# Three edits to the order of weight writes, output sums and x splits in the second MoE layer

## The chip, the cores and the metric
The kernel runs on 1 core of one Trainium2 chip. The metric is the device time of a run in microseconds (us). Before the change it is 1165.81 us, the median of 3 runs (1162.89 to 1167.37).

## The reference
Three stages follow each other, all in float32: a retention attention on 4 x 8 heads of 768 steps, a first MoE layer with w_in and w_out, and a second MoE layer with a gate. The change touches the second layer only (3072 tokens, 512 features, 1536 hidden):

```python
def _moe2_ref(x, w_gate, w_val, w_out):
    gate = 1.0 / (1.0 + np.exp(-(x @ w_gate)))
    val = x @ w_val
    return (gate * val @ w_out).astype(np.float32)
```

## The kernel before
**Precision.** TensorE (PE) multiplies a reduced form of float32. Each operand is therefore split into a high part `h` (a rounding copy on ACT) and a low part `l` (raw minus `h`, a subtraction on DVE or POOL), and each product is three matmuls: h times h, h times l, l times h.

**Seven products instead of eight.** A block of the gate or value product is cut into 2 x 2 quarters and computed with seven products of sums (a Strassen-Winograd scheme). The operands A11, A12, S1 to S4, A22 are weight quarters and their sums; B11, B21, B22, B12 and T1 to T4 are quarters of x and their differences. `product()` is one of the seven: six matmuls of 128 x 128 by 512 columns. One block is a *chain*: `begin(n)` runs A11 B11 into bank `pa` and lets ACT copy the bank to `m` (L707); `middle(n)` runs A12 B21 into `pb`, S2 T2 onto `pa` (ACT copies it to `u`, L725), S1 T1 into `pd`, S3 T3 onto `pa` (copied again, L737); `finish(n)` runs A22 T4 and S4 B22. PE works on `pa` again only when ACT has copied it.

**Groups.** The 3072 tokens are three groups of 1024. A group has twelve chains: three rounds r of two pairs p, each with a gate chain (m = 0) and a value chain (m = 1); over the rounds the six pairs q count the output weights. Group 0 (L1163) also makes the weights: `load_chain(n)` loads raw weights (L563, SP queue), `sums(n)` forms S1 to S4 on POOL (L569 to L573), `split_chain` splits them (ACT L608, DVE or POOL L609), and `keep_chain(n)` writes the four split tiles (`oh`, `ol`, early and late) to the scratch tensor `wcd` (L591), from where the groups 1 and 2 load them (L600). The tiles of a chain alternate between two sets, so a split for chain n+2 overwrites those of chain n. `load_out` loads w_out blocks (L775, two buffers `wor`), `split_out2` splits them (ACT L781, POOL L782).

**Outputs.** At the end of a round PE runs the output products; beside them `keep_out` writes split output weights, and generators on the list `todo`, made by `out_sums(q)`, load two raw w_out blocks of pair q (L808), form four quarter sums on POOL (L804), split them (ACT L822, DVE L823) and write them to `wtd` (L826). Groups 1 and 2 load them from there with `load_wt` (L834).

**x of the next group.** `prep_x(g)` is a generator that loads eight quarters of x, forms the differences T1 to T4 on POOL (L525) and splits all of them, `h` on ACT (L529), `l` on DVE, the one of T4 on POOL (L530). It is stepped at the last pair of a group, inside the last chain and between the output products. The split tiles of x exist once, so the splits wait for the old group's last products.

**What sets the order.** Each engine, and SP with its DMA queue, works its instructions off in program order, and waits at one hold everything behind it. The order is written out by hand, by the place of the calls and by stepping generators. In the lists of order below, the lines of the changed program are some 50 higher (L591 is L642, L563 is L614, L775 is L826, L608 is L659, L822 is L873, L707 is L758).

Of the kernel before, what the change touches and what calls it, by code (L numbers as in the profile page):

```python
# [8 lines left out]
F32 = mybir.dt.float32  # L9
F32R = mybir.dt.float32r  # L10
# [3 lines left out]
ALU = mybir.AluOpType  # L14

P = 128
# [9 lines left out]
def retention_moe_moe2(  # L26
# [12 lines left out]
    nc = tc.nc  # L39
# [420 lines left out]
    B11, B21, T2, T1, T3, T4, B22, B12 = range(8)  # L460
    chains = [(g, r, p, m) for g in range(NG) for r in range(NR) for p in range(PAIRS) for m in range(2)]
    NC0 = 2 * PAIRS * NR
    QS = PAIRS * NR
# [3 lines left out]
    p2 = {}  # L467
# [28 lines left out]
    def prep_x(g):  # L496

        hl = [
            [p2["x"].tile([P, 2, 512], F32R, name=f"{n}{j}", tag=f"{n}{j}") for n in ("xoh", "xol")] for j in range(7)
        ]  # L500
        xo[g] = hl
        raws = [{}, {}]

        def load(k, *js):
            for j in js:
                half, kk = {B11: (0, k), B12: (1, k), B22: (1, k + 2), B21: (0, k + 2)}[j]
                name = "xu" if g and k and j != B21 else "xt"
                raws[k][j] = p2[name].tile([P, 512], F32, name=name, tag=name)
                nc.sync.dma_start(out=raws[k][j], in_=x2d[2 * g + half][:, kk, :])

        load(0, B11, B12, B22, B21)
        if g:
            load(1, B11, B12, B22)
        yield
        for k in range(2):
            raw = raws[k]
            if k:
                if not g:
                    load(1, B11, B12, B22, B21)
                    yield  # L520
            for j in (T1, T2):
                raw[j] = p2["xt"].tile([P, 512], F32, name="xt", tag="xt")

            def diff(j, a, b):
                nc.gpsimd.tensor_tensor(out=raw[j], in0=raw[a], in1=raw[b], op=ALU.subtract)  # L525

            def split(j, engine):
                h, l = hl[j]
                nc.scalar.copy(h[:, k, :], raw[j])  # L529
                engine.tensor_tensor(out=l[:, k, :], in0=raw[j], in1=h[:, k, :], op=ALU.subtract)  # L530

            diff(T1, B12, B11)
            split(B11, nc.vector)
            if g and not k:
                load(1, B21)
            yield
            diff(T2, B22, T1)
            split(B21, nc.vector)
            yield
            raw[T3] = raw[B12]  # L540
            diff(T3, B12, B22)
            split(T2, nc.vector)
            yield
            raw[T4] = raw[B21]
            diff(T4, B21, T2)
            split(T1, nc.vector)
            yield
            split(T3, nc.vector)
            yield
            split(T4, nc.gpsimd)  # L550
            split(B22, nc.vector)
            yield

    wraw8, wo = {}, {}

# [31 lines left out]
    def keep_chain(n):  # L587

        for late in (False, True):
            for t, sl in parts[n, late]:  # L590
                nc.sync.dma_start(out=wcd[n][:, sl, :], in_=t.bitcast(F32))  # L591
# [118 lines left out]
    def middle(n):  # L710

        a, m1 = cb[n]
        b, d = bank2("pb"), bank2("pd")
        ahead = n + 1 < NC0
        if ahead and (n + 1) not in early:
            early[n + 1] = split_chain(n + 1, False)
        product(n, b, A12, B21, True, True)
        add(b, b, m1)
        while carried:
            next(carried.pop())  # L720
        c11 = consume(n, 0, b)
        next(c11)
        product(n, a, S2, T2, False, True)
        u2 = tmp("u2", 1)
        nc.scalar.copy(u2, a)  # L725
        if whole:
            whole.pop()
            split_out2()
        next(c11)
        if ahead:  # L730
            early.pop(n + 1)()
        pump()
        product(n, d, S1, T1, True, True)
        product(n, a, S3, T3, False, True)
        u3, c22 = tmp("u3", 1), tmp("c22", 1)
        pump()
        nc.scalar.copy(u3, a)  # L737
        next(c11)
        add(c22, d, u3)
        pump()  # L740
        cb[n] = [a, d, u2, c22]
# [200 lines left out]
    with tc.manual_schedule():  # L942
# [220 lines left out]
        for n, (g, r, p, m) in enumerate(chains[:NC0]):  # L1163
            last = 2 * p + m == 2 * PAIRS - 1
            more = n + 1 < NC0
            keep_chain(n)
            load_chain(n + 2)
            if more:
                load_out(n + 1)
            else:  # L1170
                load_split(n + 1)
            if not last and r == NR - 1 and p == PAIRS - 1:
                xs = prep_x(g + 1)
                next(xs)
            middle(n)
            if n + 2 < NC0 and not (last and r == NR - 1):
                sums(n + 2)
            if last:
                for _ in range(2):
                    next(xs, None)  # L1180
            if not last:
                begin(n + 1)
                rest = split_chain(n + 1, True)
                finish(n, False)
                rest()
                whole.append(n)
                continue
            rest = split_chain(n + 1, True) if more else lambda: None
            split_out2()
            ob = {}  # L1190
            for tt in range(2):
                ob[tt] = bank2("po")
                out_products(ob[tt], tt, range(2))
            finish(n, True)
            rest()
            if not more:
                load_split(n + 2)
            ob[2] = bank2("po")
            out_products(ob[2], 2, range(2))
            keep_out(r)  # L1200
            if r < NR - 1:
                todo.extend(out_sums(q) for q in ((0, 1), (2, 3, 4))[r])
            for tt in range(TOK):
                if tt >= 3:
                    ob[tt] = bank2("pd" if tt < 5 else "po")
                out_products(ob[tt], tt, range(0 if tt >= 3 else 2, FR))
                evict(g, r, tt, ob[tt])
                if tt < TOK - 1:
                    next(xs, None)
                    next(xs, None)  # L1210
                for _ in range(2):
                    while todo and next(todo[0], True):
                        todo.popleft()
                if tt == 4 and n + 2 < NC0:
                    early[n + 2] = split_chain(n + 2, False)
            for _ in xs:
                pass
            begin(n + 1)

        open_seven()  # L1220
        for g in range(1, NG):
            for q in range(QS):
                n = NC0 * g + 2 * q
                more = n + 2 < len(chains)
                if q == QS - 1 and more:
                    xs = prep_x(g + 1)
                    next(xs)
                middle(n)
                if q == 0:
                    begin(n + 1)  # L1230
                    finish(n, False)
                else:
                    seven = out_seven(q - 1)
                    next(seven)
                    finish(n, True)
                    next(seven)
                    begin(n + 1)
                load_split(n + 2)
                load_wt(q)
                middle(n + 1)  # L1240
                if q < QS - 1:
                    begin(n + 2)
                    finish(n + 1, False)
                    load_split(n + 3)
                    continue
                for _ in range(2):
                    next(xs, None)
                ob = {}
                for tt in range(2):
                    ob[tt] = bank2("po")  # L1250
                    out_pair(ob[tt], tt, (0,), True, False)
                finish(n + 1, True)
                load_split(n + 3)
                next(xs, None)
                next(xs, None)
                for tt, kind in ((2, "po"), (3, "pb")):
                    ob[tt] = bank2(kind)
                    out_pair(ob[tt], tt, (0,), True, False)
                for tt in range(TOK):
                    if tt < 4:  # L1260
                        out_pair(ob[tt], tt, (1,), False, True)
                    else:
                        ob[tt] = bank2(("pa", "pd", "po", "po")[tt - 4])
                        out_pair(ob[tt], tt, (1, 0), True, True)
                    evict(g, NR - 1, tt, ob[tt])
                    next(xs, None)
                for _ in xs:
                    pass
                begin(n + 2)
# [83 lines left out]
```

## Time and profile before
| | |
|---|---|
| median of 3 runs | 1165.81 us (1162.89, 1165.81, 1167.37) |
| profiled execution | 1164.25 us, its span 1162.3 us |
| PE busy | 1145.8 us, 99% |
| DVE, ACT, POOL busy | 764.7, 571.6, 522.0 us |
| mean granted clock | 0.998 |

How to read it: the span is the profiled part of the execution, first to last instruction. Rows give start and duration in us; in brackets stands the idle time just before an instruction and what ended it. Matmuls are pipelined: one lasts 0.39 us in the records, and starts of neighbours are what counts. Group 0 of the second layer begins near 614 us, its three output parts end near 677, 738 and 801 us, and the border from group 1 to group 2 lies near 965 to 985 us.

### The profile page before, as it was taken

What the parts mean: (1) busy time and instruction counts of PE and PEld (TensorE: products, weight loads), DVE (VectorE), ACT (ScalarE), POOL (GpSimd) and SP (SyncE); (2) the same over time, 40 slices, a digit from 0 to 9 for tenths busy, and PEclk for the clock granted to TensorE, in tenths of its full rate; (3) what the DMA queues carried; (4) which work ended last, traced back from release to release, by engine and by line L of the source; (5) the groups of instructions that cost most, each with busy time, mean ns of one, the idle gap of its engine ahead of it and who ended that gap; (6) DMA issues with size and microseconds to landing.
All of it is one profiled execution on the core that took longest, in us unless ns stands there. A gap on an engine that the chain in (4) does not pass through costs nothing.

```text
span 1162.3 us, 17446 instructions
## 1 busy us (share of the span) xinstructions
PE 1145.8 (99%) x6416; PEld 956.8 (82%) x6416; DVE 764.7 (66%) x1033; ACT 571.6 (49%) x1017; POOL 522.0 (45%) x402
## 2 busy tenths in 40 slices
PE   9999999999999999999999999899999998999998
PEld 8777888888888888888887888788888886888887
DVE  6878768676666567654555546466577778566675
ACT  4566655555555555555554454353433334543331
POOL 4568775454344444434553646373233334222220
PEclk9999999999999999999999999999999999999999
DMA  9746737443343444122006676787655574755532
GB/s 349 267 146 204 231 110 226 171 166 118 118 155 118 135 138 144 56 73 61 12 28 261 237 278 237 267 283 269 231 189 192 187 253 160 262 191 190 191 127 109
DMA packets 82849, 207.46 MB, mean 178 GB/s; under 512 B 9162, under 2 KB 13770, under 8 KB 82764
## 3 DMA queue, kind: packets, MB, share of 16 engines
q1 hardware_dynamic: 82320, 205.95, 51.9%
q8 instruction: 50, 0.82, 0.3%
q10 hardware_dynamic: 444, 0.40, 0.1%
q14 instruction: 35, 0.29, 0.1%
HBM read 147.86 MB, written 58.46 MB: 178 GB/s over the span
## 4 chain that ended last, share of the span: by engine, by line
PE 87%; DMA 3%; DVE 3%; POOL 2%; ACT 2%; issue 2%; SPq 1%; DVEq 0%; POOLq 0%; ACTq 0%
PE pa L617 15%; PE pd L617 7%; PE acc L431 7%; PE h L325 7%; PE h L327 7%; PE h L326 7%; PE acc L433 7%; PE acc L432 7%; PE po L844 6%; PE pb L617 4%; PE h L133 2%; DMA in_t<-in_qkv_dram 1%; PE h L191 1%; PE pa L844 1%; PE pd L844 1%
## 5 line engine op out<-in xcount | busy, mean ns | idle before, releaser
L310 POOL TENSOR_TENSOR wl<-wraw,wh 128x512 fp32r<-128x512 f32 x108 | 151.2, 1406 | 201.9 <-ACT wh L309 201.2
L325 PE MATMUL h<-xh,wh 128*128 128x512 f32 x380 | 149.3, 393 | 0.0
L327 PE MATMUL h<-xh,wl 128*128 128x512 f32 x380 | 148.0, 389 | 0.0
L326 PE MATMUL h<-xl,wh 128*128 128x512 f32 x380 | 147.9, 389 | 0.0
L642 POOL TENSOR_TENSOR raw<-raw,raw 128x512 f32<-128x512 f32 x40 | 62.7, 1590 | 185.5 <-DVE raw L673 159.5
L431 PE MATMUL acc<-gh,wh 128*128 128x512 f32 x368 | 145.2, 395 | 0.8 <-DVE half L446 0.8
L336 DVE TENSOR_TENSOR sg<-h,sg 128x512 f32<-128x512 f32 x92 | 63.5, 690 | 123.7 <-ACT sg L335 123.6
L433 PE MATMUL acc<-gl,wh 128*128 128x512 f32 x368 | 143.4, 390 | 0.0
L432 PE MATMUL acc<-gh,wl 128*128 128x512 f32 x368 | 143.2, 389 | 0.0
L344 DVE TENSOR_TENSOR gl<-sg,gh 128x512 fp32r<-128x512 f32 x92 | 93.0, 1011 | 53.4 <-ACT gh L343 52.2
L335 ACT ACTIVATE sg<-h 128x512 f32<-128x512 f32 x92 | 55.1, 598 | 134.5 <-PE h L327 134.5
L617 PE MATMUL pa<-xoh,oh 128*128 128x512 f32 x288 | 113.3, 393 | 7.0 <-ACT m L707 5.9
L309 ACT CAST wh<-wraw 128x512 fp32r<-128x512 f32 x188 | 109.9, 616 | 18.1 <-PE acc L433 16.9
L617 PE MATMUL pa<-xol,oh 128*128 128x512 f32 x288 | 112.9, 392 | 0.2 <-DVE xol L530 0.2
L617 PE MATMUL pa<-xoh,ol 128*128 128x512 f32 x288 | 112.7, 391 | 0.0
L343 ACT CAST gh<-sg 128x512 fp32r<-128x512 f32 x92 | 57.0, 620 | 70.3 <-DVE sg L336 68.7
L325 PEld LDWEIGHTS h<-xh,wh 128*128 128x128 f32 x380 | 71.3, 188 | 15.6 <-issue 0.7
L326 PEld LDWEIGHTS h<-xl,wh 128*128 128x128 f32 x380 | 71.3, 188 | 15.4 <-issue 0.7
L327 PEld LDWEIGHTS h<-xh,wl 128*128 128x128 f32 x380 | 71.3, 188 | 15.1 <-POOL wl L310 0.3
L431 PEld LDWEIGHTS acc<-gh,wh 128*128 128x128 f32 x368 | 69.0, 188 | 16.9 <-ACT wh L309 1.1
L433 PEld LDWEIGHTS acc<-gl,wh 128*128 128x128 f32 x368 | 69.1, 188 | 14.6
L432 PEld LDWEIGHTS acc<-gh,wl 128*128 128x128 f32 x368 | 69.1, 188 | 14.0
(232 smaller groups left out, 2708.0 us busy)
## 6 DMA issues: line engine op xcount, KB each, us to landing
w<-in_w_dram SPq DMA_DIRECT2D x68, 512.0 KB, 3.7
in_t<-in_qkv_dram SPq DMA_DIRECT2D x95, 256.0 KB, 4.4
oh<-wcd SPq DMA_DIRECT2D x24, 512.0 KB, 4.0
ol<-wcd SPq DMA_DIRECT2D x24, 512.0 KB, 4.7
w2d<-cva SPq DMA_DIRECT2D x36, 256.0 KB, 2.1
oh<-wcd SPq DMA_DIRECT2D x24, 384.0 KB, 3.4
ol<-wcd SPq DMA_DIRECT2D x24, 384.0 KB, 3.8
half<-half SPq DMA_DIRECT2D x24, 256.0 KB, 4.9
```

What stands on the lines that cost most here:

```text
L309: nc.scalar.copy(wh, raw)
L310: lo_engine.tensor_tensor(out=wl, in0=raw, in1=wh, op=ALU.subtract)
L325: nc.tensor.matmul(bank[:, :n], wh[:, k, :], xh[:, k, :n], start=(k == 0), stop=False)
L326: nc.tensor.matmul(bank[:, :n], wh[:, k, :], xl[:, k, :n], start=False, stop=False)
L327: nc.tensor.matmul(bank[:, :n], wl[:, k, :], xh[:, k, :n], start=False, stop=(k == KC - 1))
L336: nc.vector.tensor_tensor(out=sg[:, :n], in0=bank[:, :n], in1=sg[:, :n], op=ALU.mult)
L344: nc.vector.tensor_tensor(out=gl[:, :n], in0=sg[:, :n], in1=gh[:, :n], op=ALU.subtract)
L431: nc.tensor.matmul(a, wh[:, wc], gh[:, :n], start=st, stop=False)
L432: nc.tensor.matmul(a, wl[:, wc], gh[:, :n], start=False, stop=False)
L433: nc.tensor.matmul(a, wh[:, wc], gl[:, :n], start=False, stop=sp)
L617: nc.tensor.matmul(bank, w[:, kk], x[:, k, :], start=start and k == 0 and w is wh and x is xh, stop=stop and k == 1 and w is wl, skip_grou ...
L844: nc.tensor.matmul(bank[:, t * 256:(t + 1) * 256], a[:, sl], b[:, w, :], start=start and not t and a is gh and b is wh, stop=a is gl, skip ...
```

## The change
First, `keep_chain(n)` moves in group 0 from ahead of `load_chain(n + 2)` to behind `middle(n)`. Second, the second round's outputs run `out_sums` for two pairs instead of three; the fifth pair's generator goes onto `todo` for group 1 and is stepped there twice per pair q. Third, at the border of groups 1 and 2 a new generator `prep_late` takes the place of `prep_x`: all eight loads at once, six differences in two steps inside the last pair, then the splits in another order, with `l` shared between POOL and DVE.

```diff
@@ new generator, beside prep_x
+    def prep_late(g):
...
+        for k in range(2):
+            for j, half, kk in ((B11, 0, k), (B12, 1, k), (B22, 1, k + 2), (B21, 0, k + 2)):
+                raws[k][j] = tile1("raw7" if k and j == B21 else "xu" if k else "xt")
+                nc.sync.dma_start(out=raws[k][j], in_=x2d[2 * g + half][:, kk, :])
+        yield
...
+        for k in range(2):
+            raw = raws[k]
+            for j in (T1, T2):
+                raw[j] = p2["ct"].tile([P, 512], F32, name="ct", tag="ct") if k else tile1("xt")
+            diff(k, T1, B12, B11)
+            diff(k, T2, B22, T1)
+            raw[T3] = raw[B12]
+            diff(k, T3, B12, B22)
+            yield
+        for j in (B11, B21):
+            for k in range(2):
+                split(k, j, nc.gpsimd)
+            yield
+            yield
+        for k in range(2):
+            split(k, T2, nc.vector)
+        for k in range(2):
+            raws[k][T4] = raws[k][B21]
+            diff(k, T4, B21, T2)
+        yield
+        for j in (T1, T3, T4, B22):
+            for k in range(2):
+                split(k, j, nc.gpsimd if k else nc.vector)
+                yield
@@ group 0
-            keep_chain(n)
             load_chain(n + 2)
             if more:
                 load_out(n + 1)
...
             middle(n)
+            keep_chain(n)
...
-                todo.extend(out_sums(q) for q in ((0, 1), (2, 3, 4))[r])
+                todo.extend(out_sums(q) for q in range(2 * r, 2 * r + 2))
@@ groups 1 and 2
         open_seven()
+        todo.append(out_sums(QS - 2))
...
-                if q == QS - 1 and more:
-                    xs = prep_x(g + 1)
+                border = q == QS - 1 and more
+                if border:
+                    xs = prep_late(g + 1)
                     next(xs)
...
                     finish(n, True)
+                    if border:
+                        next(xs)
                     next(seven)
                     begin(n + 1)
+                    if border:
+                        next(xs)
+                        steps.append(xs)
                 load_split(n + 2)
                 load_wt(q)
+                if todo:
+                    next(todo[0], None)
                 middle(n + 1)
                 if q < QS - 1:
                     begin(n + 2)
                     finish(n + 1, False)
                     load_split(n + 3)
+                    if todo and next(todo[0], True):
+                        todo.popleft()
                     continue
-                for _ in range(2):
-                    next(xs, None)
...
-                next(xs, None)
+                steps.clear()
                 next(xs, None)
...
+                next(xs, None)
```

The order on SP's queue at the start of group 0, where place 1 of the prediction lies (`raw8` are raw weights of one chain, `wor` a raw w_out block, `oh` and `ol` the split tiles). Before:

```order
L591 DMA wcd0_138<-oh0_6036 128x1024
L591 DMA wcd0_138<-ol0_6037 128x1024
L591 DMA wcd0_138<-oh1_6126 128x768
L591 DMA wcd0_138<-ol1_6127 128x768
L563 DMA raw8_6292<-w2d_137 128x2x256
L563 DMA raw8_6292<-w2d_137 128x512
L775 DMA wor_6295<-w2d_137 128x512
L591 DMA wcd1_139<-oh0_6299 128x1024
```
The same place of SP's queue after the change:

```order
L614 DMA raw8_6288<-w2d_137 128x2x256
L614 DMA raw8_6288<-w2d_137 128x512
L826 DMA wor_6291<-w2d_137 128x512
L642 DMA wcd0_138<-oh0_6036 128x1024
L642 DMA wcd0_138<-ol0_6037 128x1024
L642 DMA wcd0_138<-oh1_6126 128x768
L642 DMA wcd0_138<-ol1_6127 128x768
L614 DMA raw8_6374<-w2d_137 128x2x256
```
The raw weights of chain 2 now stand where the four writes of chain 0 stood, and these come behind the `wor` load of chain 1.

The order on ACT at the end of the second round (`xt` are tiles of `out_sums`, `oh0` the early tile of a chain's split, `m1` the copy in `begin`). Before:

```order
L822 CAST xt_7268<-xt_7265 128x512
L822 CAST xt_7291<-xt_7288 128x512
L608 CAST oh0_7295<-raw8_7092 128x1024
L822 CAST xt_7335<-xt_7318 128x512
L822 CAST xt_7358<-xt_7341 128x512
L707 COPY m1_7371<-pa_7364 128x512
```
The same place on ACT after the change:

```order
L873 CAST xt_7241<-xt_7231 128x512
L873 CAST xt_7268<-xt_7265 128x512
L873 CAST xt_7291<-xt_7288 128x512
L659 CAST oh0_7295<-raw8_7088 128x1024
L758 COPY m1_7349<-pa_7342 128x512
```
The two copies of the fifth pair between `oh0` and `m1` are gone; they stand in group 1 now, each behind an `m1` copy there.

The order on POOL at the border of groups 1 and 2 (`xt`, `xu`, `ct` and the new `raw_9280` hold raw x and its differences, `xol` the low halves). Before:

```order
L857 TENSOR_TENSOR part<-ct,part 128x2x256 x2
L525 TENSOR_TENSOR xt<-xt 128x512 x4
L530 TENSOR_TENSOR xol_9263<-xt,xoh_9262 128x512
L525 TENSOR_TENSOR xt<-xu 128x512
L525 TENSOR_TENSOR xt<-xu,xt 128x512
L525 TENSOR_TENSOR xu<-xu 128x512
L525 TENSOR_TENSOR xt<-xt 128x512
L530 TENSOR_TENSOR xol_9263<-xt,xoh_9262 128x512
```
The same place on POOL after the change:

```order
L573 TENSOR_TENSOR xt<-xt 128x512 x3
L908 TENSOR_TENSOR part<-ct,part 128x2x256 x2
L573 TENSOR_TENSOR ct<-xu 128x512
L573 TENSOR_TENSOR ct<-xu,ct 128x512
L573 TENSOR_TENSOR xu<-xu 128x512
L578 TENSOR_TENSOR xol_9253<-xt,xoh_9252 128x512
L578 TENSOR_TENSOR xol_9253<-xu,xoh_9252 128x512
L578 TENSOR_TENSOR xol_9255<-xt,xoh_9254 128x512
L578 TENSOR_TENSOR xol_9255<-raw_9280,xoh_9254 128x512
L573 TENSOR_TENSOR xt<-xt 128x512
L573 TENSOR_TENSOR raw_9280<-raw_9280,ct 128x512
L578 TENSOR_TENSOR xol_9259<-ct,xoh_9258 128x512
```
Six differences now stand around the output addition `part<-ct`, three on each side; behind them four subtracts, the two differences of T4, and four more subtracts.

## Rows read from the trace of the kernel before
**Rows 1.** Page, part 1: busy us, share of the span, instructions.
```profile
PE 1145.8 (99%) x6416; PEld 956.8 (82%) x6416; DVE 764.7 (66%) x1033; ACT 571.6 (49%) x1017; POOL 522.0 (45%) x402
```

**Rows 2.** Waits of PE: line, releaser, us in total, times, longest.
```profile
PE pa L617 <- ACT m L707: 5.9, 2, 3.6
...
PE pa L617 <- ACT u L725: 1.1, 1, 1.1
PE po L902 <- DVE g7l L684: 0.9, 1, 0.9
```

**Rows 3.** Chain of waits near 960: start us, us, what.
```profile
960.48 1.36 PE pd L617 x6
```

**Rows 4.** PE's timeline near 629: start us, us, tile [idle before <-releaser].
```profile
629.09 0.39 PE L617 MATMUL pd<-xoh,ol 128*128 128x512 f32 x1
630.56 0.50 PE L617 MATMUL pa<-xoh,oh 128*128 128x512 f32 x1 [1.09 <-ACT u L725]
```

**Rows 5.** PE's timeline near 738.
```profile
738.02 0.39 PE L617 MATMUL pb<-xoh,ol 128*128 128x512 f32 x1
742.00 0.80 PE L617 MATMUL pa<-xoh,oh 128*128 128x512 f32 x1 [3.59 <-ACT m L707]
...
744.73 0.52 PE L617 MATMUL pd<-xoh,oh 128*128 128x512 f32 x1
```

**Rows 6.** Windows: us, busy (x count) by engine, PEclk, DMA share, GB/s.
```profile
735.00:747.00 12.00, 8.41 (x32) 6.53 (x31) 4.70 (x6) 2.81 (x5) 2.82 (x4) 0.86 0.70 258
```

**Rows 7.** Windows, border of groups 1 and 2.
```profile
968.20:984.65 16.45, 12.84 (x50) 8.56 (x49) 15.69 (x19) 8.21 (x15) 10.21 (x8) 1.00 0.35 126
```

**Rows 8.** PE's timeline near 984.
```profile
984.70 0.50 PE L617 MATMUL pa<-xoh,oh 128*128 128x512 f32 x1 [2.33 <-ACT m L707]
```

**Rows 9.** Chain of waits near 620.
```profile
616.95 0.44 SPq L591
...
621.36 4.86 DMA raw<-w2d
```

**Rows 10.** ACT's timeline near 628.
```profile
628.49 1.06 ACT L608 CAST oh<-raw 128x1024 fp32r<-128x1024 f32 x1 [3.44 <-POOL raw L570]
...
629.93 0.58 ACT L725 COPY u<-pa 128x512 f32<-128x512 f32 x1
```

**Rows 11.** Line L782: durations ns min/median/max.
```profile
L782 POOL TENSOR_TENSOR wol<-wor,woh x10: 1293/2032/2240, 631.1 to 765.7; 128x512 fp32r<-128x512 f32 x10
```

**Rows 12.** Line L591, the wcd writes.
```profile
DMA to landing us min/median/max: 2.3/4.6/8.7
```

**Rows 13.** SP's timeline near 650.
```profile
651.82 0.32 SPq L775 DMA_DIRECT2D wor<-w2d  x1
```

**Rows 14.** Windows, end of group 0.
```profile
768.00:800.00 32.00, 32.00 (x142) 26.48 (x142) 25.27 (x32) 15.12 (x27) 19.80 (x13) 1.00 0.95 344
```

**Rows 15.** Chain of waits near 738.
```profile
734.78 2.92 DMA xt<-w2d
...
740.84 0.62 ACT xt L822
```

**Rows 16.** POOL's timeline near 662 and 965.
```profile
662.55 2.96 POOL L804 TENSOR_TENSOR xt<-xt 128x256 f32<-128x256 f32 x4 [2.71 <-DMA xt<-w2d]
...
965.34 4.55 POOL L525 TENSOR_TENSOR xt<-xt 128x512 f32<-128x512 f32 x3 [10.94 <-issue]
```

**Rows 17.** ACT's timeline near 677.
```profile
677.23 0.59 ACT L707 COPY m<-pa 128x512 f32<-128x512 f32 x1 [0.77 <-PE pa L617]
```

**Rows 18.** DVE's timeline near 965.
```profile
965.72 1.78 DVE L673 TENSOR_TENSOR raw<-c,sg 128x512 f32<-128x512 f32 x1
```

**Rows 19.** ACT's timeline, 960 to 973.
```profile
960.57 0.59 ACT L725 COPY u<-pa 128x512 f32<-128x512 f32 x1 [2.13 <-PE pa L617]
...
972.38 2.71 ACT L529 CAST xoh<-xt 128x512 fp32r<-128x512 f32 x5
```

**Rows 20.** Line L673, window 800 to 960: ns min/median/max.
```profile
L673 DVE TENSOR_TENSOR raw<-c,sg x5: 692/693/694, 818.8 to 935.5; 128x512 f32<-128x512 f32 x5
```

**Rows 21.** Line L525, second layer: ns min/median/max.
```profile
L525 POOL TENSOR_TENSOR xt<-xt x10: 1267/1304/1740, 776.4 to 981.7; 128x512 f32<-128x512 f32 x10
```

More of the change, by code (lines that the diff above doesn't have):

```diff
@@ L552, in prep_x, with tile1, diff, split @@
             yield
+    def prep_late(g):
+        hl = [
+            [p2["x"].tile([P, 2, 512], F32R, name=f"{n}{j}", tag=f"{n}{j}") for n in ("xoh", "xol")] for j in range(7)
+        ]
+        xo[g] = hl
+        raws = [{}, {}]
+        def tile1(name):
+            return p2[name].tile([P, 512], F32, name=name, tag=name)
+        for k in range(2):
[3 more added lines that the diff above has]
+        yield
+        def diff(k, j, a, b):
+            raw = raws[k]
+            nc.gpsimd.tensor_tensor(out=raw[j], in0=raw[a], in1=raw[b], op=ALU.subtract)
+        def split(k, j, engine):
+            h, l = hl[j]
+            nc.scalar.copy(h[:, k, :], raws[k][j])
+            engine.tensor_tensor(out=l[:, k, :], in0=raws[k][j], in1=h[:, k, :], op=ALU.subtract)
+        for k in range(2):
+            raw = raws[k]
+            for j in (T1, T2):
[20 more added lines that the diff above has]
+                yield
     wraw8, wo = {}, {}
```

## The prediction
> **What bounds the kernel now.** I read the page's busy shares first: TensorE (PE) is busy 1145.8 of 1162.3 us, 99% [rows 1]. The matmuls set the time, and a change that adds and removes none can only win back moments in which PE stands still. Next come PE's waits: 5.9 us in two places for a copy of bank `pa` to `m`, and 0.9 for `g7l` [rows 2]. PE's timeline says where they lie and what each costs. Six matmuls of 512 columns take 1.36 us [rows 3], 0.227 each; what exceeds that is lost.
> Place 1, first chain border of group 0: behind the matmul at 629.09 the next should start at 629.32 and starts at 630.56, having waited for ACT's copy `u` [rows 4]: 1.24.
> Place 2, end of the second round of outputs: behind 738.02 the next starts at 742.00 instead of 738.25 [rows 5], 3.75. Those six take until 744.73, 2.73 instead of 1.36, 1.37 more: 5.12 in all. The granted clock of this stretch averages 0.86 [rows 6]: after 3.59 idle PE ran at the lower level, 1.2 GHz, for a while.
> Place 3, border of groups 1 and 2: 50 matmuls in 968.20 to 984.65 [rows 7]; 50 x 0.227 = 11.35 of 16.45, so 5.1 are lost. The last piece is 2.33 idle for `m` at 984.70 [rows 8], the clock staying full.
> The three hold 11.5 us, about all that this change can regain.
>
> **Part 1: raw weights ahead of the four `wcd` writes.** The chain of waits of place 1: SP starts the writes at 616.95, the second raw load leaves at 621.36 and lands 4.86 later [rows 9], POOL sums it, ACT splits it, and only then copies `u`. Issued where the first write stands, the load leaves some 4 us sooner, with 1.8 MB less in front. 1.24 is needed: place 1 goes, **+1.24**.
> What is late next: ACT's split for chain n+2 overwrites the tile from which `wcd(n)` is written, and `wcd(n)` now stands on SP behind the load of `wor`, which waits for a buffer that POOL's L782 frees. In five of the twelve chains (1, 2, 5, 6, 9) that comes from inside the chain. From the start M of its A12 product: `u` can be copied at M+2.8 and holds ACT about 0.6 [rows 10], the copy L781 behind it another 0.62 (as long as an L822 [rows 15]), M+4.0; L782 takes 1.29 to 2.24 [rows 11]; two issues on SP of 0.44 [rows 9] reach M+6.2 to M+7.1; landing takes 4.6 in the median [rows 12]: M+10.8 to M+11.7. The next chain starts at M+9.5 (seven products of 1.36). It needs its `u` 4.08 later, so the split (1.06, then one more copy, then `u` at 0.58 [rows 10]) may start until about 2.0 after it, M+11.5. Median landings come 0.7 before that or 0.2 behind: I charge 0 (at most 5 x 0.2 = 1.0). The longest landing is rival C.
> At the end of a round the writes move as well, from ahead of the raw load to behind it: 1.8 MB closer to the loads of the output weights. In the first round SP issues the `wor` load at 651.82 [rows 13]; by the tiles' shapes 0.25 + 1.8 + 1.5 + 0.5 = 4.05 MB then stand up to the first pair's loads, 11.8 us at the 344 GB/s of the crowded stretch [rows 14], 663.6. Before, POOL began these sums at 662.55 [rows 16]: 1.0 late. The `m` copy behind them has 1.5 of room: ACT was idle 0.77 before it [rows 17], and PE wants it one product of 1.36 after the bank is full, 0.78 more than the copy takes. So 0; the other end is rival B.
>
> **Part 2: the fifth pair's output sums.** Its load leaves at 734.78, its last split is on ACT at 740.84, and `m` follows [rows 15]. Without it ACT goes from the fourth pair's splits over one L608 to `m`, as the second piece of order shows, and `m` is copied when the bank is full: place 2 goes, **+5.12**. The work comes back in group 1: two loads, four 256-wide POOL operations, two ACT copies of 0.62, two DVE subtracts, four writes. The two ACT copies stand behind an `m` copy, where ACT then waits about 2.1 for PE, as at 960.57 [rows 19]; POOL's stand among idle time. So 0; without that cover 2 x 0.62 = 1.2.
>
> **Part 3: x of the third group.** Before, seven POOL differences, two POOL subtracts and twelve DVE subtracts lie around the last products of group 1. The clearest harm: DVE's `raw<-c,sg` takes 1.78 at 965.72 [rows 18], 0.69 in earlier chains [rows 20], while POOL runs differences. That makes `g7h` and `g7l` late: the 0.9 of rows 2 and smaller waits around it, some 1.5 of the 5.1 (the 2.33 for `m` leave 2.8 for all others). Now six differences run earlier on POOL, in what was 10.94 idle [rows 16], and no split stands on ACT ahead of the last `g7h` copy: this piece goes. The eighth x load needs a buffer that a DVE split frees and holds the weight loads behind it on SP; those are for a chain two periods (19 us) off: 0.
> The rest depends on when ACT reaches `m`: behind 14 copies, two of which wait for POOL's `T4` differences, which stand behind four POOL subtracts (third piece of order). The x copies behind the last `g7h` start at 972.38 before [rows 19], 1.5 sooner without the delays, 970.9; the first ends 0.54 later, and POOL starts at 971.4. Six operations at 1.30 end at 979.2, at 1.74 at 981.8, the median and the longest of one row [rows 21]. Then ACT has three copies at 0.54 (five in 2.71 [rows 19]) and `m`, 2.25: `m` is out at 981.5 to 984.1. Without any delay PE would go on at 984.70 - 5.1 = 979.6. So of the 5.1 come back 0.6 to 3.2. DVE does four of its six subtracts in that time; if each costs POOL 0.3 of the 0.44 between median and longest, the six end at 980.4 and `m` is out at 982.65: **+2.0**.
> The Trainium skill, SBUF — State Buffer, section Who interferes with whom, says that a DVE instruction with two SBUF inputs and a GpSimd instruction that reads SBUF lock each other out. The trace agrees: 1.78 against 0.69, 1.74 against 1.30. The rule speaks against giving POOL eight subtracts beside DVE's six: by it POOL's whole row may run at 1.74, and this part would give 0.6 instead of 2.0.
>
> **The sum.** 1.24 + 5.12 + 2.0 = 8.4. The profiled execution took 1164.25 (the span of 1162.3 and 1.95 around it) and becomes 1155.85. The median of the three runs, 1165.81, lies 1.56 above it: the forecast is 1157.4, its own range 1155 to 1159.5. 0.5%, 5.8 us, is what a measurement of this kernel can tell from no change: faster is under 1160.0, slower over 1171.6.
>
> **The rivals.**
> A. Only part 2 pays in full. POOL runs at 1.74 throughout (part 3 gives 0.6), and at place 1 the wait passes from the raw load to a `wcd` write in one of the next chains (part 1 gives 0). For it: rows 18 and the tight M+11.7. Against it: half of DVE's subtracts are gone. 1165.8 - 5.1 - 0.6 = 1160.1.
> B. The `wcd` writes delay the output weights. With all 1.8 MB in the way, 5.1 at 344 GB/s, the first round is 5.1 - 1.5 = 3.6 late, as long as the idle of place 2, so with its 1.4 of lower clock 5.0. In the second round a pair fewer, at least 740.84 + 0.62 - 734.78 = 6.7, leaves 3.75 - 6.7 + 5.1 = 2.1 late or less. Some 6.5 of the 8.4 are lost again: 1163.9. It decides from 1.5 us of delay. Against it: these writes were ahead of the same loads before.
> C. The other side: the writes land late. If they take the row's longest, 8.7 [rows 12], each of the five chains waits 8.7 less the 4.9 that fit (the middle of 11.5 - 7.1 and 11.5 - 6.2), 3.8, with 1.4 of lower clock behind it: 5 x 5.2 = 26.0 less 8.4, 1183; without the clock 1176. It eats the whole gain from landings of 4.9 + 8.4/5 = 6.6 on. Against it: 8.7 is the extreme of 48 writes, and the most crowded stretch, 768 to 800 [rows 14], lies behind all five.
> D. The change does not do what it says: the new x generator joins a list whose first entry is an exhausted one, which alone is asked, and so in the order no x split lies inside the last chain. The forecast counts them all behind it; were they spread, all 11.5 could go, 1154.3.
>
> **How the numbers follow.** Forecast 0.64, D 0.04, A 0.16, B 0.08, C 0.05, and 0.03 for an unseen loss that leaves no change. Faster: the forecast, D and half of A, 0.76. Same: the other half of A, B and the last, 0.19. Slower: 0.05. The range runs from D's all regained, 1154, less 0.5, to B, 1163.5; C and the last stay outside.
>
> **What would show it.** Place 1 right: SP's raw loads ahead of the `wcd` writes, no wait for `u` near 630. Place 2: no wait over 0.5 for `m` near 738, the granted clock full there. Place 3: no `g7l` wait near 970, one wait for `m` of 1 to 3.5, POOL's subtracts between 1.30 and 1.74. New waits to look for: ACT's L659 held by a `wcd` write (A, C), `m` at the end of the first round (B). I am wrong if PE's waits for `m` and `u` sum to over 5 us.

## The result, and the profile after

The changed kernel takes 1156.7 us (median of 6 runs, 1154.74 to 1158.69) against 1166.91 us (6 runs, 1162.89 to 1167.73). The ratio is 0.9919, with a 95% interval from 0.9902 to 0.9936: 7.5 to 11.4 us faster, clear of the 0.5% bound. The forecast was 1157.4, in a range from 1153.5 to 1163.5. The time was right. Of its three terms the second held, the third had the idle right and the clock behind it wrong, and the first came to nothing.

The profiled executions differ by less than the medians: 1164.25 to 1157.72, spans 1162.3 to 1156.0. The mean granted clock explains part of it: over later runs of the kernel before it lies between 0.995 and 0.998, and the profiled one had 0.998, the top of that; the profiled run of the changed kernel has 0.998 in a kernel whose runs go from 0.998 to 1.000. By this clock the trace of before shows less time lost than most of its executions, and that of the changed kernel as much as any of its own.

The page of the changed kernel, its part 1 (busy us, share of the span, instructions; answers to [rows 1]):

```profile
PE 1145.0 (99%) x6416; PEld 957.8 (83%) x6416; DVE 756.0 (65%) x1027; ACT 571.0 (49%) x1017; POOL 530.8 (46%) x408
```

PE is busy for as long as before, in a span 6.3 us shorter. In PE's waits of the changed kernel this one alone is left behind 600 us (answers to [rows 2]; line, releaser, us in total, times, longest):

```profile
PE pa L668 <- ACT m L758: 3.9, 2, 2.8
```

The `u` wait of place 1 [rows 4] and the `g7l` wait [rows 2] are gone, and of the two waits for `m` the one of place 2 [rows 5] is gone too. But `m` is still waited for twice, 3.9 us in all: once in a place where nobody waited before. PE's timeline of the changed kernel at the end of the first round and at the border of groups 1 and 2 (start us, us, tile, idle time before and what ended it):

```profile
677.37 0.39 PE L668 MATMUL pb<-xoh,ol 128*128 128x512 f32 x1
678.86 0.50 PE L668 MATMUL pa<-xoh,oh 128*128 128x512 f32 x1 [1.09 <-ACT m L758]
...
977.58 0.50 PE L668 MATMUL pa<-xoh,oh 128*128 128x512 f32 x1 [2.83 <-ACT m L758]
...
979.21 0.63 PE L668 MATMUL pa<-xoh,ol 128*128 128x512 f32 x1
979.64 0.63 PE L668 MATMUL pd<-xoh,oh 128*128 128x512 f32 x1
```

At 678.86 PE starts 1.26 later than the 677.60 that 677.37 and 0.23 make: a new stall, in the first round. At 977.58 there are 2.83 idle (2.33 in [rows 8]), and from 978.4 on the matmuls start 0.43 apart instead of 0.23, for eight of them. The windows view of that stretch (us, busy by engine in the order PE, PEld, DVE, ACT, POOL, then PEclk, DMA share, GB/s) has the clock at 0.53:

```profile
978.70:982.00 3.30, 3.30 (x9) 2.55 (x8) 0.73 (x2) 1.09 (x2) 2.49 (x2) 0.53 0.00 0
```

So place 3 lost 5.1 before and 4.7 after (3.0 at the wait, 0.1 behind it, 1.6 at the lower clock). The products of gate and value ahead of the border are no longer drawn out: the line that took 1.78 [rows 18] takes 0.69, as in other chains [rows 20]; POOL does nothing beside it now. DVE's timeline of the changed kernel:

```profile
959.87 0.69 DVE L724 TENSOR_TENSOR raw<-c,sg 128x512 f32<-128x512 f32 x1
```

What makes `m` late is POOL's row of six, and ACT behind it. POOL's timeline of the changed kernel there (the second of the six, 1.30 like the first, is left out):

```profile
965.91 1.31 POOL L578 TENSOR_TENSOR xol<-xt,xoh 128x512 fp32r<-128x512 f32 x1 [13.41 <-ACT xoh L577]
...
968.41 1.76 POOL L578 TENSOR_TENSOR xol<-xt,xoh 128x512 fp32r<-128x512 f32 x1
970.13 1.74 POOL L578 TENSOR_TENSOR xol<-raw,xoh 128x512 fp32r<-128x512 f32 x1
971.84 1.74 POOL L573 TENSOR_TENSOR xt<-xt 128x512 f32<-128x512 f32 x1
973.53 1.83 POOL L573 TENSOR_TENSOR raw<-raw,ct 128x512 f32<-128x512 f32 x1
```

ACT's timeline in the same stretch:

```profile
973.61 0.62 ACT L577 CAST xoh<-xt 128x512 fp32r<-128x512 f32 x1 [3.09 <-POOL xt L573]
975.39 0.62 ACT L577 CAST xoh<-raw 128x512 fp32r<-128x512 f32 x1 [1.16 <-POOL raw L573]
...
976.96 0.57 ACT L758 COPY m<-pa 128x512 f32<-128x512 f32 x1
```

The first two subtracts take 1.30, the next four operations 1.74 to 1.83. ACT stands 3.09 and 1.16 before its copies of the two `T4` differences; two copies later it reaches `m`.

The new stall of the first round is followed back in three timelines of the changed kernel, with lines of the kernel before beside them. SP's:

```profile
650.54 0.32 SPq L826 DMA_DIRECT2D wor<-w2d  x1
...
654.23 1.14 SPq L847 DMA_DIRECT2D wtd0h<-woh  x1
655.40 0.99 SPq L847 DMA_DIRECT2D wtd0l<-wol  x1
...
660.97 0.93 SPq L859 DMA_DIRECT2D xt<-w2d  x2
```

The same of SP in the kernel before, behind its `wor` load at 651.82 [rows 13]:

```profile
652.18 0.43 SPq L796 DMA_DIRECT2D wtd0h<-woh  x1
...
658.44 2.35 SPq L808 DMA_DIRECT2D xt<-w2d  x2
```

POOL's, where the sums begin:

```profile
664.71 2.95 POOL L855 TENSOR_TENSOR xt<-xt 128x256 f32<-128x256 f32 x4 [6.19 <-DMA xt<-w2d]
```

ACT's, up to the copy `m`:

```profile
675.77 0.62 ACT L873 CAST xt<-xt 128x512 fp32r<-128x512 f32 x1 [0.77 <-POOL xt L855]
676.30 1.05 ACT L659 CAST oh<-raw 128x1024 fp32r<-128x1024 f32 x1
677.25 1.06 ACT L977 COPY part<-po 128x512 f32<-128x512 f32 x2
678.20 0.60 ACT L758 COPY m<-pa 128x512 f32<-128x512 f32 x1
```

In the kernel before, that last split on ACT, and on PE the matmul that is at 677.37 in the changed kernel:

```profile
673.88 0.62 ACT L822 CAST xt<-xt 128x512 fp32r<-128x512 f32 x1 [0.78 <-POOL xt L804]
```

```profile
678.16 0.39 PE L617 MATMUL pb<-xoh,ol 128*128 128x512 f32 x1
```

The writes of `wcd` now stand between 650.54 and 654.23. From the `wor` load to the first loads of the sums SP needs 10.4 instead of 6.6. POOL's first sums begin at 664.71 instead of 662.55 [rows 16], 2.2 late; the last split, which `m` stands behind on ACT, comes at 675.77 instead of 673.88, 1.9 late, although PE itself is 0.8 earlier here. ACT goes from the last split over L659 and two evictions to `m` without a pause, where it had 0.77 of rest [rows 17].

### The profile page after: what moved, and what is told of

Read it like the earlier page. It is cut to its first block, busy times and chain, and to the rows that moved or that the text cites. A ratio compares the mean times of both kernels' runs of the same rounds, so it can differ in the third digit from the quotient of the medians.

```text
span 1156.0 us, 17422 instructions
## 1 busy us (share of the span) xinstructions
PE 1145.0 (99%) x6416; PEld 957.8 (83%) x6416; DVE 756.0 (65%) x1027; ACT 571.0 (49%) x1017; POOL 530.8 (46%) x408
## 4 chain that ended last, share of the span: by engine, by line
PE 90%; DMA 2%; POOL 2%; ACT 2%; DVE 2%; issue 1%; SPq 1%; DVEq 0%; POOLq 0%; ACTq 0%
PE pa L668 16%; PE pd L668 8%; PE acc L431 7%; PE h L325 7%; PE h L326 7%; PE h L327 7%; PE acc L433 7%; PE acc L432 7%; PE po L895 6%; PE pb L668 4%; PE h L133 2%; DMA in_t<-in_qkv_dram 1%; PE h L191 1%; PE pa L895 1%; PE pd L895 1%
```

## The experiments

Ten kernels were run. Each ratio is against runs of the kernel before on the same chip; where two versions are compared with each other, both medians are given.

### One part alone

**Part 1 alone.** The kernel before with `keep_chain(n)` moved, nothing else:

```diff
-            keep_chain(n)
             load_chain(n + 2)
...
             middle(n)
+            keep_chain(n)
```

> Part 1 alone on the kernel before. My theory (the parts act as local stalls that add up; in the trace of the changed kernel part 1 took away 1.24 us at the first chain border, but left 0.31 for a copy of u at the next one and 1.36 for the m copy at the end of the first round): place 1 gone, 0.3 and 1.4 new, and with three pairs still in the second round place 2 grows by the 1 to 2 us by which the output weights come later, 5.1 to about 6.5. Net slower by 1 to 2.5 us: about 1168.5 against 1166.9. Rival (the recorded forecast: the writes have room): faster by 1.2, no wait for m at the end of the first round, place 2 unchanged.

Measured: 1167.86 us (11 runs) against 1166.01, ratio 1.0020 (1.0011 to 1.0029): slower by 1.3 to 3.4 us. PE's timeline of this kernel, at the first and second end of a round:

```profile
677.38 0.50 PE L617 MATMUL pa<-xoh,oh 128*128 128x512 f32 x1 [0.18 <-ACT m L707]
...
744.25 0.80 PE L617 MATMUL pa<-xoh,oh 128*128 128x512 f32 x1 [6.65 <-ACT m L707]
```

There is no wait for `u` near 630. The wait at place 2 grew from 3.59 [rows 5] to 6.65, with a longer spell of the lower clock behind it. The idle at the end of the first round is 0.18 here and 1.09 in the changed kernel; over the four traces with this order (these two, and two below with 0.42 and 0.74) it is 0.2 to 1.1. The rival, that the writes have room there, is refuted: they cost more at a round's end than the 1.24 they bring at place 1.

**Part 2 alone.**

```diff
-                todo.extend(out_sums(q) for q in ((0, 1), (2, 3, 4))[r])
+                todo.extend(out_sums(q) for q in range(2 * r, 2 * r + 2))
...
         open_seven()
+        todo.append(out_sums(QS - 2))
```

> Part 2 alone on the kernel before. My theory: place 2 (3.6 idle for m and 1.4 of lower clock) goes whole, the work in group 1 costs nothing: 5.1 us faster, about 1161.8, PE's longest wait for m near 738 under 0.5. Rival (part 2 carries nearly all of the 10 us by which the medians differ, since place 2 is longer in other executions than in the profiled one): 8 to 10 us faster, 1157 to 1159.

Measured: 1159.07 us (5 runs), ratio 0.9941 (0.9928 to 0.9953): 5.5 to 8.4 us faster. PE's waits in this kernel:

```profile
PE pa L617 <- ACT m L707: 2.3, 1, 2.3
PE pa L617 <- ACT u L725: 1.7, 2, 1.2
```

ACT's timeline near 738 in this kernel:

```profile
737.80 0.59 ACT L707 COPY m<-pa 128x512 f32<-128x512 f32 x1 [3.46 <-PE pa L617]
```

ACT waits 3.46 for PE before `m`, where PE waited 3.59 for `m`: place 2 is gone whole, and with it the lower clock. The one wait for `m` left is that of place 3. The two waits for `u` are that of place 1, 1.20 here, and a new one of 0.55 at 700.71, in the second round, that the forecast did not have. The spans of the two profiled runs differ by 5.5; 0.8 of it lies behind the last matmul, where the programs are alike, and from the layer's first matmul to its last it is 4.5: place 2 less some 0.8 for the two waits for `u`. The medians differ by 6.9. The rival's 8 is inside the interval, so how much of the excess is place 2 in other executions isn't settled by this. That the copies in group 1 cost nothing is seen in the waits: none is new there.

**Part 3 alone.** `prep_late` in place of `prep_x` at the border, and the two other edits undone.

> Part 3 alone on the kernel before. My theory: the waits for g7h and g7l near 970 go (2.1 us), but m comes about 2.8 us late, PE then runs about eight matmuls at the lower clock (1.6 us), so only 0.4 us are won: 1166.5. Rival (the recorded forecast: same idle, clock staying full): 2 us faster, 1164.9, no spell of matmuls 0.43 apart behind the idle.

Measured: 1161.24 us (5 runs, 1160.21 to 1164.61), ratio 0.9963 (0.9949 to 0.9977): 2.7 to 5.9 us faster, more than either theory. PE's timeline at the border in this kernel:

```profile
981.07 0.50 PE L668 MATMUL pa<-xoh,oh 128*128 128x512 f32 x1 [2.84 <-ACT m L758]
```

The windows view of the same stretch (PEclk is the third number from the end):

```profile
981.00:984.50 3.50, 3.44 (x15) 2.85 (x16) 0.78 (x2) 1.10 (x3) 3.50 (x3) 1.00 0.00 0
```

The idle for `m` is 2.84, as long as in the changed kernel to 0.01, but here the clock stays at 1.00 and neighbours start 0.23 apart. So the lower clock behind this wait isn't set by the idle alone: it is there in the changed kernel and not here, at the same place behind the same wait. It is there too, behind 2.83 each, in the two traces below that leave this place as it is: the change without part 1 and, with a clock of 0.53 from 976.6 to 980.0, the version with the last writes late. The window of the change without part 1:

```profile
978.40:982.00 3.60, 3.60 (x10) 2.82 (x9) 0.00 (x0) 1.08 (x2) 2.67 (x3) 0.53 0.00 0
```

The kernel before is alike: in its trace the clock stays full behind 2.33 idle [rows 8], and in that of part 2 alone too (1.00 from 980.0 to 984.5). The window of the kernel before:

```profile
984.70:989.00 4.30, 4.30 (x19) 3.59 (x20) 3.85 (x6) 1.01 (x2) 0.29 (x1) 1.00 0.54 191
```

In the run of part 1 alone, where that stretch of the program is the same, the clock falls. PE's timeline there:

```profile
987.50 0.61 PE L617 MATMUL pa<-xoh,oh 128*128 128x512 f32 x1 [2.33 <-ACT m L707]
```

And the window behind that start:

```profile
987.50:992.00 4.50, 4.50 (x13) 3.54 (x14) 3.85 (x6) 1.19 (x2) 0.29 (x1) 0.62 0.46 175
```

With the same 2.33 idle the clock of the next 4.5 us averages 0.62. What a wait here costs is therefore a length plus, in four of these seven traces, a lower clock of some 1.6 us. Every kernel has one trace, so that this differs between executions of one kernel is read from the mean clocks: a trace without such a spell has 1.000, with one 0.998 or 0.999, with two (part 1 alone) 0.995. The runs of the changed kernel go from 0.998, the profiled one, to 1.000 at 1154.74, its fastest. Those of the kernel before go from 0.995 to 0.998, as if some had the spell of place 3 beside that of place 2; none of them has a trace, so this is not shown.

The trace also says where the excess over 2.0 may come from. Of the 3.8 by which its span is shorter, 2.0 lie at place 3; 0.5 lie at place 1 (0.54 idle instead of 1.09) and 0.3 at place 2 (3.07 idle instead of 3.59, with a little more of the lower clock), places that this edit does not touch.

**The change without part 1.**

> The changed kernel without part 1 (writes back ahead of the raw load). My theory: place 1 comes back (1.24 lost), but the waits near 639 (0.31) and at the end of the first round (1.36) go: 0.4 us faster than the changed kernel, about 1156.3. Rival (the recorded forecast: part 1 is worth 1.24): 1.2 us slower than the changed kernel, about 1158.

Measured: 1156.44 us (5 runs), ratio to the kernel before 0.9914 (0.9901 to 0.9928), against 1156.70 and 0.9919 with part 1. In the trace the wait for `u` is back (1.1) and that at the end of the first round is gone, as PE's waits in this kernel show:

```profile
PE pa L668 <- ACT m L758: 2.8, 1, 2.8
...
PE pa L668 <- ACT u L776: 1.1, 1, 1.1
```

By the times part 1 is worth nothing that these intervals, 1.6 and 2.0 us to each side, let one see; by the traces, what it gives at place 1 it takes at the end of the first round.

### The border of groups 1 and 2

**POOL without DVE beside it.** DVE writes zeros where it subtracted its six low halves at that border; this part of the third group's x is left out.

```diff
+            if engine is nc.vector:
+                engine.memset(l[:, k, :].bitcast(F32), 0.0)
+                return
             engine.tensor_tensor(out=l[:, k, :], in0=raws[k][j], in1=h[:, k, :], op=ALU.subtract)
```

> The changed kernel, where DVE writes zeros into its six low halves at the last border instead of subtracting (left out: the low halves of T2 and of one half of T1, T3, T4 and B22 in the third group); POOL's order is the same. Theory one (POOL's operations are slow there because DVE instructions with two SBUF inputs run beside them): POOL's six operations ahead of m take 1.30 each, 7.8 instead of 9.4, and the idle for m shrinks from 2.83 to about 1.2. Rival (they are slow for another reason, the DMA writes or their operands): still 1.7 for the later four, idle near 2.8.

Measured: one run, 1153.11 us. POOL's timeline at the border in this kernel:

```profile
967.32 1.30 POOL L581 TENSOR_TENSOR xol<-xt,xoh 128x512 fp32r<-128x512 f32 x1
968.58 1.30 POOL L581 TENSOR_TENSOR xol<-raw,xoh 128x512 fp32r<-128x512 f32 x1
969.83 1.31 POOL L573 TENSOR_TENSOR xt<-xt 128x512 f32<-128x512 f32 x1
971.07 1.31 POOL L573 TENSOR_TENSOR raw<-raw,ct 128x512 f32<-128x512 f32 x1
```

PE's timeline behind the `m` copy:

```profile
974.61 0.50 PE L671 MATMUL pa<-xoh,oh 128*128 128x512 f32 x1 [0.96 <-ACT m L761]
```

The four operations that took 1.74 to 1.83 take 1.30, and the idle for `m` falls from 2.83 to 0.96. The operands and transfers of POOL are the same, so it is DVE's two-input subtracts that draw POOL's operations out by 0.44 to 0.5 each, 1.9 in the four.

**Two subtracts moved from POOL to DVE.**

```diff
-                split(k, j, nc.gpsimd)
+                split(k, j, nc.gpsimd if j == B11 else nc.vector)
```

> The changed kernel with the low halves of B21 subtracted on DVE, so that POOL reaches the two differences of T4 after two subtracts instead of four. My theory (the m copy at the border of groups 1 and 2 is late because POOL's six operations of 1.3 to 1.8 us stand ahead of ACT's last copies): two operations of about 1.75 less, T4 ready 3.5 us sooner, ACT's 14 copies then run back to back and m is out in time: idle for m under 0.3 and no matmuls at the lower clock behind it; 3 us faster than the changed kernel, 4.7 where that one had the lower clock: about 1153. Rival (it is DVE and the shared load of DVE and POOL that limits, so that moving work to DVE only moves the wait): PE waits 1.5 us or more there, for xol of T2 or still for m; within 1.5 us of the changed kernel.

Measured: 1153.45 us (4 runs), ratio to the kernel before 0.9908 (0.9893 to 0.9923). By medians that is 3.25 less than the changed kernel, by the two ratios 1.3, whose intervals overlap; the runs of the kernel before were 2 us faster in this set. Two versions below, measured side by side, differ by this edit alone: 1155.16 and 1152.56, 2.6. The mean clock is 1.000 in all runs. POOL's timeline in this kernel:

```profile
967.24 1.75 POOL L573 TENSOR_TENSOR xt<-xt 128x512 f32<-128x512 f32 x1
968.95 1.83 POOL L573 TENSOR_TENSOR raw<-raw,ct 128x512 f32<-128x512 f32 x1
```

PE's waits in this kernel:

```profile
PE pa L668 <- ACT u L788: 0.9, 1, 0.9
...
PE pa L668 <- ACT m L758: 0.4, 1, 0.4
```

POOL's operations are as long as before, 1.75 and 1.83, but the second `T4` difference ends at 970.8 instead of 975.4. The wait for `m` at the border is gone (the 0.4 stand at the end of the first round), and no spell of the lower clock is left. A wait of 0.9 for a later copy `u` took its place, with 0.3 for a copy `xoh` ahead of it: the length of the chain ahead of `m` counted, and the rival, that the wait only moves, has 1.2 of it.

### The end of the rounds

**The last chain's writes behind the loads of the output weights**, for the first two rounds:

```diff
             middle(n)
-            keep_chain(n)
+            if not last or not more:
+                keep_chain(n)
...
+                if tt == 3 and more:
+                    keep_chain(n)
                 if tt == 4 and n + 2 < NC0:
```

> The changed kernel with the four wcd writes of the last chain of rounds one and two issued behind the loads of the output weights, between the output products. My theory (these 1.8 MB in front of the loads made m late at the end of the first round): the output sums start about 2 us sooner, the 1.1 us of idle for m near 679 goes, 1.4 us faster: about 1155.3. Rival (the loads are late for the kept output weights ahead of them, whatever the wcd writes do): idle for m stays near 1.1, time unchanged at 1156.7.

Measured: 1155.16 us (5 runs), ratio 0.9919 (0.9906 to 0.9931): by the median 1.5 less than the changed kernel, by the ratio the same. The time alone doesn't settle it, the trace does. POOL's timeline at the end of the first round in this kernel:

```profile
661.01 2.95 POOL L855 TENSOR_TENSOR xt<-xt 128x256 f32<-128x256 f32 x4 [3.56 <-DMA xt<-w2d]
```

ACT's timeline there:

```profile
675.85 0.59 ACT L758 COPY m<-pa 128x512 f32<-128x512 f32 x1 [0.77 <-PE pa L668]
```

POOL's first sums begin at 661.01 instead of 664.71, and ACT has its 0.77 of rest before `m` again, as before the change [rows 17]. PE's wait there is gone. The rival, that the kept output weights delay the loads, is refuted.

**Both last edits together.**

> Both of the last two edits together on the changed kernel. My theory: local stalls that add up; all waits for m behind 600 us under 0.4 each, 1.4 + 3 to 4.7 faster than the changed kernel: 1151.5. Rival (one of the edits gains nothing): 1153 to 1155.5.

Measured: 1152.56 us (4 runs), ratio 0.9896 (0.9883 to 0.9910): side by side 0.9 less than with B21 on DVE alone and 2.6 less than with the writes late alone, and no run of this version is as slow as the fastest of either; so both edits gain, together 1.0 less than I expected. The largest wait left behind 600 us is the 0.9 for `u` that moving B21 had brought. DVE's timeline ahead of it in this kernel:

```profile
975.34 2.37 DVE L578 TENSOR_TENSOR xol<-xt,xoh 128x512 fp32r<-128x512 f32 x2
977.64 0.69 DVE L708 TENSOR_TENSOR pb<-pb,m 128x512 f32<-128x512 f32 x1
```

ACT's sigmoid stands ahead of that copy and waits for the add at 977.64, which stands behind two subtracts of 2.37 together.

**One of these two subtracts on POOL as well.**

```diff
-                split(k, j, nc.gpsimd if k else nc.vector)
+                split(k, j, nc.gpsimd if k or j == B22 else nc.vector)
```

> The last version (B21 on DVE, wcd writes late) with both low halves of B22 on POOL. In that version 0.9 us of idle for u are left at 979: ACT's sigmoid ahead of that copy waits for DVE's add, which stands behind two subtracts of 2.37 us together. My theory: with one subtract less ahead of it the add ends about 1.1 us sooner and this idle goes, 1 us faster: about 1151.5. Rival (POOL has five subtracts in a row behind the T4 differences, the last then ends near 979, and the remaining DVE subtract is drawn out by them): the same idle, 1152.6, or a new wait of PE for xol of B22.

Measured: 1151.41 us (4 runs), ratio 0.9888 (0.9871 to 0.9904), the best of all, against 0.9919 of the changed kernel and 0.9896 of the version above, measured in another set; these last two intervals overlap, so the gain over it is read from the trace. The wait for `u` is gone; in PE's waits behind 600 us only this one is left:

```profile
PE pb L668 <- ACT xoh L577: 0.3, 1, 0.3
```

**B21 on DVE, without part 1.**

> The changed kernel with B21 on DVE but without part 1. My theory: part 1 took 1.24 us away at place 1 and cost as much at the end of the first round, so without it the time is the same as with it when nothing else differs: within 0.8 us of 1153.5 (the version with B21 on DVE and with part 1), place 1 back with an idle near 1.1 and no idle for m near 678. Rival (part 1 is worth its 1.24): 1154.7 or more.

Measured: 1153.87 us (4 runs), ratio 0.9912 (0.9897 to 0.9927), against 1153.45 and 0.9908 with part 1: the same, with the wait at place 1 back at 0.8. With the round's last writes moved as well, the version with part 1 has 1152.56 and 0.9896. That is in line with part 1's own 1.2 once its cost at the end of a round is taken away, though the intervals overlap.

## Why the prediction was right, and where it wasn't

**Place 1 and the raw load: right in itself.** The wait for `u` near 630 is gone in every trace with part 1 and there (0.5 to 1.2) in every trace without it. What was costed at nothing was not: the step "1.0 late, and `m` has 1.5 of room, so 0" failed. The last split came 1.9 late, PE arrived 0.8 sooner, mostly for having lost its stall at place 1, and 2.7 less 1.5 makes 1.2 of the 1.26 that were measured. The other end, rival B, was priced at 5.1 late; less than half of that came. The delay was worked out from bytes and a mean rate. What the timelines show is SP's own time: the four issues of `wcd` take 3.3 where none stood before, and the two behind them 1.14 and 0.99 instead of 0.43 each. In the version with the last writes late these two take 0.43 again. In other traces with part 1 the idle there is less (0.18 to 0.74), so 1.26 is the upper end. In the profiled execution part 1 came out as +1.24 - 1.26 - 0.3, and by the run without it as nothing.

**What is late next: right, and close.** The estimate that median landings come 0.7 before ACT must split or 0.2 behind it: ACT now waits three times for a `wcd` write, 3.8 us in all. What ACT's split line L659 waits for, in the changed kernel (us, times):

```profile
  DMA wcd<-oh: 3.8, 3
```

The landing of the write line L642 in the changed kernel:

```profile
DMA to landing us min/median/max: 3.8/5.0/9.0
```

The median landing is 5.0 against 4.6 [rows 12], the longest 9.0: a margin of tenths. None of these waits is named in PE's: the 0.3 that PE loses at 639.33 has another cause, as ACT's timeline of the changed kernel ahead of that `u`, copied at 638.69, shows:

```profile
638.20 0.59 ACT L745 CAST g2h<-pd 128x512 fp32r<-128x512 f32 x1 [1.81 <-DVE pd L743]
```

ACT stood 1.81 for a product of DVE, not for a write. Rival C began to show and stopped short of PE.

**Place 2: right.** 5.12 was forecast, the wait and the lower clock behind it are gone from every trace with part 2, and with part 2 alone 5.5 by the spans and 6.9 (5.5 to 8.4) by the medians came, of which not all is place 2.

**Place 3: the idle right, the clock behind it wrong.** The forecast's `m` at 982.65 against 979.6 is an idle of 3.05; 3.0 were lost at the wait. The chain was the forecast's: ACT behind T4, T4 behind four subtracts. POOL's six took 9.45 (965.91 to 975.36) where I had 9.0, and ACT 2.2 behind them as worked out; POOL only started 0.5 earlier against PE. The step that failed is that no lower clock follows, since none follows in the one trace of before. In the changed kernel's trace 1.6 went to it, and 0.4 of the 2.0 was left; in that of part 3 alone the 2.0 came whole. The same program stretch as in the kernel before has the lower clock in one of three traces. By medians part 3 alone brought 4.8 (2.7 to 5.9). In its own trace 0.8 is gained at places 1 and 2, which it does not touch; where the rest of the excess over 2.0 comes from stays open, and the granted clock of the runs, up to 0.003 apart in the kernel before, is only a hint.

**The rule on shared reads: borne out, as far as it goes.** The Trainium skill, SBUF — State Buffer, section Who interferes with whom, says that a DVE instruction with two SBUF inputs and a GpSimd instruction that reads SBUF exclude each other. The trace agrees: with DVE's subtracts replaced by writes, the four drawn-out POOL operations fell from 1.74 and more to 1.30. But the time that the rule by itself forecast, all six at 1.74, did not come: two were at 1.30.

**The sum.** 8.4 was forecast. In medians parts 2 and 3 bring 6.9 and 4.8 alone and 9.6 together (the run without part 1), part 1 nothing on top, and the change 10.2. From one profiled execution to the other it is only 6.5: the places give 1.24 - 1.26 - 0.3 + 5.12 + 0.4 = 5.2, and 0.8 lies behind the last matmul, where the programs are alike. So the sum, worked out on the trace of before, was too large for the traces and too small for the medians. That 1157.4 lay 0.7 from 1156.7 is luck in part, from errors that cancel: part 1 was forecast 1.2 too good, parts 2 and 3 by medians 2.5 too small, and the kernel before, taken at 1165.81, came to 1166.91. Rival A comes nearest to what failed (part 1 gives 0). In the changed kernel's trace part 3 gives 0.4, near A's 0.6, but by the lower clock and not by POOL at 1.74 throughout; by the medians part 3 paid, and A's 1160.1 was too late. The range was to end at B, but B's own sum is 1163.9, not 1163.5.

## What to carry to other kernels

A load moved ahead of writes puts these writes ahead of something else: cost the bytes, and the time that SP's issues take, at each later place where a load is waited for, with the slack that the earlier start of everything else eats up. Where a chain decides, count the operations that stand ahead of the awaited one on each engine and move two of them to another engine, even at the price of contention: 2.6 us came from two subtracts. And read the lower clock behind an idle of 2 to 3 us as a cost that one trace has and another has not, before and after alike, so that a single trace does not price it.

## What the runs showed of the hardware

An idle of 2.33 us of PE was followed by full clock in two traces (the kernel before, part 2 alone) and by a mean of 0.62 over the next 4.5 us in a third with the same instructions there (part 1 alone). 2.83 and 2.84 likewise: the clock fell in the changed kernel (0.53 over 978.7 to 982.0), in the change without part 1 and in the version with the last writes late, and stayed at 1.00 in part 3 alone. Behind 3.59, 3.07 and 6.65 idle at place 2 the lower clock came each time. What decides in the cases between, the runs don't show.

The other thing is how evenly POOL's subtracts of 128 x 512 behind 965 fall into two lengths in the changed kernel: 1.26 to 1.31 or 1.72 to 1.83, and 1.28 to 1.31 for all ten where DVE subtracts nothing. A subtract of DVE beside one of POOL does not always lengthen POOL's: beside the 1.30 at 967.16 DVE's own, begun at 967.95, took 1.06 instead of 0.68, and beside the 1.26 at 975.32 two of DVE's, begun at 975.34, took 3.48.
